# Attention with block sums and a gated feed-forward layer: other filling products for TensorE, and a new written-out order

## The chip, the cores and the metric

The kernel runs on one core of a Trainium2 chip. The metric is the device time in microseconds of one execution, as the median of a few runs. Profiles come from one profiled execution, whose own time is given beside them.

## The reference

```python
def _attn_ref(q, k, v):                 # (4, 8, 768, 64) each
    k_sum = k.reshape(B, H, nb, 32, D).max(axis=3)
    v_sum = v.reshape(B, H, nb, 32, D).mean(axis=3)
    scores_l = scale * np.matmul(q, k.transpose(0, 1, 3, 2))
    mask_l = np.abs(pos[:, None] - pos[None, :]) < 16
    scores_s = scale * np.einsum('bhsd,bhnd->bhsn', q, k_sum) + np.log(32)
    # softmax over [masked local scores, block scores], then times [v, v_sum]
    ...
def _moe_ref(x, w_in, w_out):           # x (3072, 512), d_ff 2048
    h = x @ w_in
    g = h * np.clip(h + 3.0, 0.0, 6.0) / 6.0
    return g @ w_out
```

Each query sees the keys less than 16 places away and one maximum of k (one mean of v) for each of 24 blocks. The heads' outputs side by side are x of the feed-forward layer, whose output in float32 is the result.

## The kernel before, in words

TensorE's products are in bfloat16 with float32 sums in PSUM. Work is cut by batch (4) and half of the sequence (384 rows): eight stages s = 0 to 7 of the feed-forward layer, each fed by the attention of one half.

The operations have names with a stage in them. For batch 0, `k0` to `k3` transpose k (L391) and take block maxima and copies on VectorE and ScalarE; `q0` and `q1` do so for the second half of q (L420), `q2` and `q3` for the first (L441, from the wide load `Q0w`). `s0p0` and `s0p1` are scores of a head pair (L489): those of the half that is done first begin with a product that writes the mask into PSUM, called cover (L481), which reads the identity (`c.1`, GpSimd, L250) and a bias (`c.3`, VectorE, L261). `u0` and `u1` sum v over blocks (L535). `v0p` are the values of a head pair with their division and transposes (L581, L589); `v4hg` and `vbhg` are those of later halves (L623, L636). For later batches `w` turns k and q into place with VectorE's transposes, `s` are scores of four heads at a time (L512), `u` sums of v (L553). `Fsxf` is the first product of the layer for stage s and slice f of d_ff (four L666 products of 384 columns; ScalarE's relu, L670; VectorE's gate, L671). `Gstxa` is the second (L683, sixteen products of 512 columns in four parts, then a copy and a store).

Nothing is scheduled at run time or by a planner in the file: `ORDER` is a written-out list of all operations. `Plan.issue` reads it word by word, gives an operation its buffers when it is first named (the one of its pool that was set free longest ago), and hands it to its engine. Every engine works its part of the list in that order, and waits where an operation needs something that isn't there. A suffix `:A` or `:D` names ScalarE or VectorE where both can do it. Loads are issued by GpSimd, stores and moves by SyncE, in the order of the list too.

Words that begin with a sign are filling products: `-n` is n products of 128 columns of ones, `~n` n products of 512, into a PSUM buffer that is free. Nobody reads them. They stand where TensorE would wait, mostly in the first 23 us.

Of the kernel before, what the change touches and what calls it, by code (L numbers as in the profile page):

```python
# [36 lines left out]
s011.1 F0x4.2 F0x4.3 F0x4.4 s011.2 F0x4.5 I8.0 F0x8.0 F0x8.1 F0x8.2 F0x5.0 I0.0 F0x1.0 F0x1.1 v410.0 v410.1 v410.2 c.12:A F0x5.1  # L37
F0x5.2 F0x1.2 F0x1.3 F0x1.4 F0x11.0 F0x11.1 F0x11.2 F0x1.5 F0x7.0 F0x7.1 F0x7.2 v411.3 I12.0 F0x15.0 F0x15.1 F0x15.2 v411.4:D
F0x13.0 F0x13.1 F0x13.2 v410.3 v410.4:A F0x14.0 F0x10.0 F0x14.1 F0x14.2 F0x10.1 F0x10.2 I2.0 F0x3.0 F0x3.1 F0x3.2 F0x3.3 F0x3.4
F0x3.5 F1x4.0 F1x4.1 F1x4.2 F0x0.0 F0x0.1 F0x0.2 F0x0.3 F0x9.0 F1x2.0 F0x2.0 F0x2.1 K11.0 K10.0 K12.0 K13.0 w10.0 F0x0.4 F0x9.1  # L40
F0x9.2 F1x2.1 F0x2.2 F1x2.2 F0x0.5 F1x12.0 F1x12.1 F1x12.2 Q1w4.0 Q1w5.0 Q1w1.0 F1x5.0 F1x5.1 F1x5.2 F1x9.0 F1x9.1 F1x9.2 F0x2.3
F0x2.4 F0x2.5 F1x8.0 F1x8.1 F1x8.2 F0x6.0 F0x6.1 F0x6.2 F1x6.0 F1x6.1 F1x6.2 w11.0 Q1w3.0 q5.0 F1x14.0 q5.1:A F1x14.1 F1x14.2
F1x15.0 F1x15.1 F1x15.2 w11.1:A F1x1.0 Q1w2.0 Q1w0.0 q7.0 q7.1:A w11.2 w10.1:D w10.2 w11.3:D w10.3:D q6.0 q6.1:A F1x7.0 F0x12.0
F0x12.1 F0x12.2 q4.0 q4.1:A O0.0 F1x7.1 F1x1.1 G02x0.0 O1.0 G02x0.1 F1x1.2 F1x7.2 s100.0 s100.3 s100.1 F1x3.0 w13.0 w12.0 F1x3.1
F1x0.0 F1x0.1 F1x0.2 F1x11.0 w12.2 w12.3:D w13.2 w13.3:D s100.4 s101.0 s101.1 s101.3 O2.0 O3.0 F1x3.2 s100.2 G02x0.2 G02x0.3
G02x0.4:A w13.1:A w12.1:A F1x10.0 s101.4 G00x0.0 G00x0.1 V10.0 h100.0:A F1x11.1 s101.2 F1x11.2 h110.0:D V12.0 h130.0:D s110.0
s110.3 s110.1 G00x0.2 G00x0.3 G00x0.4:A h120.0:D s110.2 F1x10.1 u4.0 u4.1:A u4.3:D u4.2:A u4.4:D G01x0.0 G01x0.1 G01x0.2
h101.0:A h121.0:A v100.0 u4.5:D s110.4 G02x0.5 v101.0 G01x0.3 G01x0.4:A F1x10.2 F1x13.0 v100.1 v100.2 v100.3 h111.0:A G12x0.0
v101.1 v101.2 v100.4:A v101.3 v101.4:A F1x13.1 h131.0:A K21.0 G12x0.1 G12x0.2 K20.0 K22.0 K23.0 w20.0 w20.3 w21.0 F1x13.2 w21.3
# [752 lines left out]
```

## Time and profile before

| | us |
|---|---|
| median of 3 runs | 220.14 (218.53 to 221.66) |
| profiled execution, its own time | 221.35 |
| its span, first to last instruction | 219.6 |
| TensorE products busy | 212.7 (97%) |
| VectorE busy | 164.0 (75%) |
| ScalarE busy | 135.9 (62%) |
| GpSimd busy | 50.0 (23%) |

PE is TensorE's products, PEld its weight loads, DVE VectorE, ACT ScalarE, POOL GpSimd, SP SyncE. Each product has a weight load ahead of it that counts as an instruction of its own. Products are pipelined, and a product's end is modelled, so a busy TensorE need not be at its peak; how far apart products start says more. PEclk is the share of full clock that TensorE was granted. In the chain of waits, "issue" is time in which an engine waited for nothing that the profile shows.

### The profile page before, as it was taken

Reading aid. Unit: us, or ns where it says so; the run is one execution under the profiler, and the core shown is the slowest. Engines: PE = TensorE matmul, PEld = TensorE weight load, DVE = VectorE, ACT = ScalarE, POOL = GpSimd, SP = SyncE. Lnnn points to the kernel's source line nnn. Section 1 sums busy time; section 2 is a strip of 40 time slices with the busy share of each in tenths; the row PEclk is TensorE's granted clock in tenths of the full one; section 3 lists DMA queues with packets and bytes.
Section 4 is the critical chain, followed back from the end, with each engine's and each line's share of the span. In section 5 each row is a group of like instructions: output and inputs, shape, how many; then the busy total and the mean of one; then the engine's idle time right before and its main releaser. Section 6 shows DMA issues by size and latency. Waiting matters only on the chain.

```text
span 219.6 us, 6084 instructions
## 1 busy us (share of the span) xinstructions
PE 212.7 (97%) x2546; PEld 122.3 (56%) x2546; DVE 164.0 (75%) x311; ACT 135.9 (62%) x270; POOL 50.0 (23%) x66
## 2 busy tenths in 40 slices
PE   7998999999999999999999999999999999999993
PEld 7566666655445556555545555555555555554442
DVE  5888589997999999999989999968966666421111
ACT  8579497787897878893857687377244555510110
POOL 7977447824630007600000000000000000000000
PEclk9999579999999999999999999999999999999999
DMA  5999999999999915999333134023233200021332
GB/s 69 149 155 188 204 186 158 202 199 162 177 186 173 102 48 35 165 210 138 36 39 146 17 37 116 3 30 63 33 34 36 100 0 4 0 96 72 123 132 105
DMA packets 91580, 22.68 MB, mean 103 GB/s; under 512 B 82208, under 2 KB 88608, under 8 KB 91552
## 3 DMA queue, kind: packets, MB, share of 16 engines
q0 software_dynamic: 62288, 14.41, 70.8%
q1 hardware_dynamic: 29264, 7.87, 15.0%
q8 instruction: 20, 0.33, 0.6%
q14 instruction: 8, 0.07, 0.1%
HBM read 28.82 MB, written 6.29 MB: 160 GB/s over the span
## 4 chain that ended last, share of the span: by engine, by line
PE 89%; DVE 4%; DMA 3%; issue 1%; POOL 1%; ACT 1%; POOLq 0%
PE h L666 37%; PE o L683 31%; PE h L683 5%; DMA first<-in_k_dram 3%; PE S L623 3%; PE S L512 2%; PE S L489 1%; PE h L581 1%; PE S L666 1%; PE S L553 1%; PE S L636 1%; DVE at L521 1%; DVE vaug L241 1%; PE S L481 1%; DVE red L467 1%
## 5 line engine op out<-in xcount | busy, mean ns | idle before, releaser
L666 PE MATMUL h<-x,win 128*128 128x384 bf16 x496 | 90.5, 328 | 0.0
L670 ACT ACTIVATE r<-h 128x384 f32<-128x384 f32 x124 | 58.7, 491 | 37.2 <-PE h L666 36.7
L683 PE MATMUL o<-wout,g 128*128 128x512 bf16 x336 | 81.0, 380 | 0.0
L671 DVE SCALAR_TENSOR_TENSOR g<-r,h 128x384 bf16<-128x384 f32 x124 | 65.5, 548 | 20.4 <-ACT r L670 17.8
L666 PEld LDWEIGHTS <-win 128*128 128x128 bf16 x512 | 48.8, 98 | 35.3 <-issue 0.3
L683 PEld LDWEIGHTS <-g 128*128 128x128 bf16 x400 | 38.1, 98 | 38.4 <-issue 0.2
L520 ACT ACTIVATE at<-S 120x768 bf16<-120x768 f32 x24 | 18.7, 809 | 3.6 <-PE S L512 3.5
L343 POOL DMA_DIRECT2D vaug<-in_v_dram x10 | 11.8, 1186 | 20.6 <-PE S L623 18.2
L241 ACT COPY ot<-o 128x512 f32<-128x512 f32 x15 | 8.8, 586 | 11.2 <-PE o L683 11.2
L521 DVE TENSOR_TENSOR at<-at,mask 96x768 bf16<-96x768 bf16 x24 | 12.9, 546 | 1.2 <-ACT at L520 0.7
L241 DVE COPY ot<-o 128x512 f32<-128x512 f32 x6 | 4.1, 690 | 12.6 <-PE o L683 12.6
L605 DVE TENSOR_TENSOR xn<-S,rc 128x768 bf16<-128x768 f32 x14 | 13.2, 948 | 0.3
L683 PE MATMUL h<-wout,g 128*128 128x256 bf16 (+1 forms) x64 | 11.9, 326 | 0.0
L241 ACT COPY ot<-h 128x512 f32<-128x512 f32 (+1 forms) x2 | 1.0, 478 | 17.5 <-PE h L683 17.5
L467 DVE TENSOR_REDUCE red<-kaug 128x24 bf16<-128x768 bf16 x12 | 11.1, 934 | 0.1
L455 DVE STREAM_TRANSPOSE kaug<-kraw 128x768 bf16<-128x768 bf16 x8 | 8.1, 1028 | 1.1 <-PE S L512 1.1
L770 PEld LDWEIGHTS <-idle 128*128 128x128 bf16 x78 | 7.2, 127 | 2.9 <-DVE idle L287 1.1
L770 PE MATMUL o<-idle 128*128 128x128 bf16 (+1 forms) x55 | 7.4, 327 | 1.1 <-DVE idle L287 1.1
L241 ACT COPY vaug<-vaug 32x640 bf16<-32x640 bf16 (+3 forms) x17 | 8.3, 535 | 0.1
L642 DVE STREAM_TRANSPOSE y<-xn 128x768 bf16<-128x768 bf16 x8 | 7.7, 968 | 0.1
L512 PEld LDWEIGHTS <-kaug 32*128 32x128 bf16 x576 | 5.3, 93 | 4.2 <-issue 3.4
L623 PEld LDWEIGHTS <-at 120*64 120x64 bf16 x336 | 6.5, 114 | 2.1 <-issue 1.1
(108 smaller groups left out, 198.2 us busy)
## 6 DMA issues: line engine op xcount, KB each, us to landing
out_dram<-ot SPq DMA_DIRECT2D x19, 256.0 KB, 3.1
vaug<-in_v_dram POOLq DMA_DIRECT2D x6, 384.0 KB, 13.5
wout<-in_moe_w_out_dram POOLq DMA_DIRECT2D x4, 512.0 KB, 10.0
win<-in_moe_w_in_dram POOLq DMA_DIRECT2D x3, 512.0 KB, 10.3
kraw<-in_k_dram POOLq DMA_DIRECT2D x8, 192.0 KB, 12.6
x<-y SPq DMA_DIRECT2D x64, 24.0 KB, 2.0
first<-in_k_dram POOLq DMA_DIRECT2D x6, 192.0 KB, 14.6
first<-in_q_dram POOLq DMA_DIRECT2D x6, 192.0 KB, 11.5
```

What stands on the lines that cost most here:

```text
L241: {"ACT": nc.scalar.copy, "DVE": nc.vector.tensor_copy, "POOL": nc.gpsimd.tensor_copy}[eng](o, i)
L343: op("POOL", "dma128", lambda: nc.gpsimd.dma_start(out=o[BLK:WIN, a:z, 0:D], in_=rows[:, a:z]), w=[("v", b % 2, c) for c in range(lo, hi)] ...
L467: op("DVE", "max", lambda: nc.vector.tensor_reduce(red.slot[:], w[:, :, BLK:WIN].rearrange("p t (n c) -> p t n c", n=2), axis=AX.X, op=ALU ...
L520: op("ACT", "exp", lambda a=a, e=e: nc.scalar.activation(a, X[e].slot[0:KEYS, :, 0:HALF], AF.Exp, scale=scl), r=[X[e]], w=[("at", p, half)])
L521: op("DVE", "masking", lambda m=m: nc.vector.tensor_tensor(m, m, mask[:, low(half):low(half) + HQ].unsqueeze(1).to_broadcast([WIN, 2, HQ, ...
L605: nc.vector.tensor_tensor(o, src[..., 0:D], r.unsqueeze(len(r.shape)).to_broadcast(list(o.shape)), op=ALU.mult)
L623: nc.tensor.matmul(X.slot[64 * c:64 * c + 64, i, m:m + D + 1], a[:, t * QB:(t + 1) * QB], vaug[b % 2][0:KEYS, h, t, 0:D + 1], start=True, ...
L666: nc.tensor.matmul(bank(h)[:, 0:HALF], w_in_sb[:, kt, cols], xt[s].slot[:, kt], start=(kt == 0), stop=(kt == NP - 1))
L670: op("ACT", "relu", lambda: nc.scalar.activation(r.slot[:], bank(h)[:, 0:HALF], AF.Relu, bias=0.5, scale=1.0 / 6.0), r=[h], w=[r])
L671: op("DVE", "gate", lambda: nc.vector.scalar_tensor_tensor(gt[s].slot[:, ft], r.slot[:], 1.0, bank(h)[:, 0:HALF], op0=ALU.min, op1=ALU.mul ...
L683: nc.tensor.matmul(o.slot[:, a:z], gt[s].slot[:, ft, ts * 128:(ts + 1) * 128], w_out_sb[:, ft, a:z], start=(ft == 0), stop=(ft == NFT - 1))
L770: nc.tensor.matmul(o[:, 0:m * 128].rearrange("p (m c) -> p m c", m=m), idle[:], idle[:].unsqueeze(1).to_broadcast([128, m, 128]), start=Tr ...
```

## The change

Three things are changed.

1. `ORDER` is another list of the same operations. It differs from the first word to the last. Ahead of `k1`, `-44` has become `_36 -19` and two covers, `s010.0 s000.0`; the identity `c.1` now stands ahead of q's first load on GpSimd; the fill ahead of `k2` is `=8` five times and `=3` instead of `~11`; other fills have become `=` words too, and there are more of them up to `q3`.
2. Two more filling words: `_n` is n products of 64 columns, and `=n` is one product in float32 of 32 n columns, on the same ones read as float32 (`idle` is made 256 wide for that).
3. The transposes of wide q for batch 1 have a name of their own (`qwtr4`), which changes no instruction.

The diff, its lists cut to their beginnings and ends:

```diff
 ORDER = """
-c.0 c.6 K01.0 c.19 c.9:A c.10:A c.5 c.8:D c.18 c.7 c.14:A c.15:A c.17 c.11:A K00.0 K02.0 c.2 c.4 c.20 Q00.0 c.13:D c.1 -44 k1.0
-c.3 k1.1 k1.4 Q01.0 k1.2:D c.16 k0.0 k0.3:A k0.2:A k1.3:A k0.1 k0.4 ~11 k2.0 k2.3:A k3.0 k3.1 k2.1 ~2 q0.0 q0.2:A k3.4 k2.2:D
-q0.1:A s010.0 ~1 -1 s010.1 s010.2 q1.0 q1.2:D s000.0 k3.2:A V00.0 h000.0:D q1.1:D k3.3:D s000.1 s000.2 s030.0 -3 s030.1 s030.2
-V01.0 ~1 -1 u0.0 u0.1:A h010.0:D k2.4 v00.0 -3 v00.1 u0.3:A -1 v01.0 v01.1 v00.2 v00.3 u0.4:D h001.0:A h011.0:A v01.2 v01.3
-s020.0 s020.1 s020.2 V03.0 V02.0 u1.0 h030.0:D h031.0:D -2 v01.4 h020.0:D v01.5:D u1.3:A u1.4:A -2 v03.0 Q0w2.0 -4 v03.1 v03.2
-v03.3 Q0w1.0 v00.4 Q0w0.0 -2 q3.0 q3.1:D v00.5:D u1.1:A u1.2:D h021.0:A q2.0 q2.1:A v02.0 v02.1 v02.2 v02.3 s021.0 v03.4 v03.5:D
-s031.0 s021.1 s021.2 s031.1 s031.2 I4.0 F0x4.0 F0x4.1 s001.0 v02.4 s011.0 v02.5:D s001.1 s001.2 v411.0 v411.1 v411.2 u0.2:A
...
-G60x0.3 G60x0.4:D G60x0.5 G71x0.2 G71x0.3 G71x0.4:A G71x0.5
+c.0 K01.0 c.7 c.15:A c.5 c.6 c.9:A c.18 K00.0 c.11:A c.10:D c.13:D K02.0 c.14:A c.8:D c.20 c.2 c.3 c.1 _36 -19 s010.0 s000.0 c.4
+c.19 c.16 c.17 k1.0 k1.3:D k1.1 k1.4 k0.0 Q00.0 k0.2:A k0.3:A k1.2:A k0.1 k0.4 =8 =8 =8 =8 =8 =3 k2.0 k2.3:A k3.0 k3.1 k3.4 k2.1
+k3.3:D =8 q0.0 q0.1:A q0.2:A =8 =6 s000.1 s000.2 =4 s010.1 s010.2 Q01.0 q1.0 =3 s030.0 k2.2:D k2.4 V00.0 h000.0:D h001.0:D V01.0
+=8 =8 =1 u0.0 u0.3:D u0.1:D s020.0 q1.2:A k3.2:A s030.1 q1.1:A h010.0:A h011.0:A s020.1 s020.2 V02.0 u0.4:D h020.0:D v01.0 v01.1
+v00.0 v01.2 v01.3 V03.0 v00.1 v00.2 v00.3 u1.0 h030.0:D u1.3:A h031.0:D s030.2 u1.4:D h021.0:A v01.4 v01.5:D Q0w1.0 Q0w0.0
+Q0w2.0 u1.1:A =8 =8 =8 =3 q3.0 q3.1:D q2.0 u1.2:D v03.0 q2.1:A v03.1 v03.2 s021.0 s021.1 v03.3 v02.0 v02.1 v02.2 v02.3 s011.0
+s011.1 v00.4 v00.5:D v03.4 v03.5:D =2 v02.4 v02.5:A s021.2 s011.2 s031.0 s001.0 I2.0 F0x3.0 s031.1 s031.2 F0x3.1 F0x3.2 F0x3.3
+F0x3.4 F0x3.5 I4.0 F0x6.0 F0x6.1 F0x6.2 F0x4.0 F0x4.1 F0x4.2 v411.0 s001.1 v411.1 s001.2 u0.2:A v411.2 F0x4.3 F0x4.4 F0x4.5
...
+G60x0.4:A G60x0.5 G70x0.0 G70x0.1 G60x0.0 G72x0.1 G72x0.2 G70x0.2 G70x0.3 G70x0.4:A G50x0.5 G60x0.1 G60x0.2 G60x0.3 G60x0.4:D
+G70x0.5 G60x0.5 G72x0.3 G72x0.4:D G71x0.2 G71x0.3 G72x0.5 G71x0.4:A G71x0.5
 """
...
-            if token[0] in "~-":
-                keep(int(token[1:]), 4 if token[0] == "~" else 1, min(...))
+            if token[0] in "~-_=":
+                keep(int(token[1:]), "-~_=".index(token[0]), min(...))
...
-    idle = sb([128, 128], BF16, "idle")
+    idle = sb([128, 256], BF16, "idle")
...
-        op("PE", "qwtr", tr, ...)
+        op("PE", "qwtr4" if b else "qwtr", tr, ...)
...
     def keep(n, m, o):
         o = o[:, 0] if any(o is x for x in pairs) else o[:]
+        if m == 3:
+            w = idle[:].bitcast(F32)
+            nc.tensor.matmul(o[:, 0:32 * n].rearrange("p (n c) -> p n c", n=n), w, w[:, 0:32].unsqueeze(1).to_broadcast([128, n, 32]), start=True, stop=True)
+            return
+        c = (2, 8, 1)[m]
         for _ in range(n):
-            nc.tensor.matmul(o[:, 0:m * 128].rearrange("p (m c) -> p m c", m=m), idle[:], idle[:].unsqueeze(1).to_broadcast([128, m, 128]),
+            nc.tensor.matmul(o[:, 0:c * 64].rearrange("p (c x) -> p c x", c=c), idle[:, 0:128], idle[:, 0:64].unsqueeze(1).to_broadcast([128, c, 64]),
                              start=True, stop=True)
```

More of the change, by code (lines that the diff above doesn't have):

```diff
@@ L38 @@
[L38 to L49, printed above, removed]
@@ new lines @@
+F0x11.2 v410.2 c.12:A F0x7.0 F0x7.1 F0x7.2 v411.3 I12.0 F0x15.0 F0x15.1 F0x15.2 F0x13.0 F0x13.1 F0x13.2 v410.3 K13.0 v410.4:A
+v411.4:D F0x10.0 F0x10.1 F0x10.2 F0x14.0 F0x14.1 F0x9.0 F0x9.1 F0x2.0 F0x14.2 F0x0.0 F0x0.1 F0x0.2 F0x0.3 F0x2.1 F0x0.4 K11.0
+K10.0 K12.0 w10.0 F0x9.2 F1x14.0 F1x14.1 F1x14.2 F1x1.0 F1x1.1 F0x2.2 F0x2.3 F0x2.4 F1x1.2 F0x2.5 F0x0.5 F1x5.0 F1x5.1 F1x5.2
+F1x4.0 F1x4.1 F1x4.2 F1x2.0 F1x2.1 F1x2.2 w10.2 w10.3:D Q1w5.0 Q1w0.0 Q1w1.0 Q1w2.0 q7.0 q7.1:A q6.0 q6.1:A F1x7.0 F1x7.1 F1x7.2
@@ new lines @@
+F2x5.1 F2x5.2 s111.3 w22.3 F2x3.0 F2x3.1 F2x3.2 G12x0.3 G12x0.4:A w23.0 F2x9.0 F2x9.1 F2x9.2 s111.4 s111.1 F2x12.0 F2x12.1
+F2x12.2 G10x0.0 w23.2:A F2x11.0 F2x11.1 K32.0 H2.0 h131.0:A V20.0 V22.0 H2.1:D G10x0.1 s111.2 Q20.0 K31.0 w23.3 F2x15.0 F2x15.1
+F2x15.2 F2x11.2 F2x13.0 u5.0 u5.1:A F2x13.1 v111.0 v110.0 w23.4:A w21.4:A u5.2:A F2x10.0 F2x4.0 G10x0.2 G10x0.3 w20.4:A F2x13.2
+G02x0.5 Q22.0 Q32.0 v111.1 F2x2.0 u5.5:D v110.1 v110.2 G01x0.5 G12x0.5 G00x0.5 K33.0 Q23.0 w20.1 v111.2 u5.3:D w21.1 w22.2:A
@@ new lines @@
+G10x0.4:A G10x0.5 v110.3 w22.4:A F2x2.1 F2x10.1 v110.4:A F2x10.2 G11x0.0 G11x0.1 F2x4.1 F2x4.2 u5.4:D w22.1 K30.0 v111.3
+v111.4:A F2x2.2 G11x0.2 G11x0.3 G11x0.4:A F3x0.0 F3x0.1 F3x0.2 w23.1 F3x8.0 F3x8.1 F3x8.2 s200.0 s200.1 s200.3 s200.4 G22x0.0
+F3x7.0 F3x7.1 F3x7.2 F2x14.0 F2x14.1 F2x14.2 s210.0 s200.2 F3x13.0 F3x4.0 F2x8.0 s210.3 s210.4 s210.1 s210.2 G22x0.1 F3x13.1
+F3x13.2 F3x4.1 F3x4.2 F2x8.1 F2x8.2 v201.0 v201.1 v200.0 v200.1 v200.2 F3x6.0 F3x6.1 F3x6.2 G22x0.2 G22x0.3 G22x0.4:A F3x2.0
@@ new lines @@
+F3x2.1 w21.5:A v200.3 v201.2 w20.5:D v201.3 F3x3.0 F3x12.0 F3x3.1 F3x12.1 F3x12.2 s201.0 F3x2.2 F3x3.2 V32.0 H3.0 V30.0 H3.1:A
+Q30.0 Q33.0 Q31.0 w30.0 G20x0.0 w23.5:A s201.1 F3x14.0 F3x14.1 s201.2 G20x0.1 s201.3 F3x9.0 F3x1.0 G20x0.2 w31.0 F3x14.2 F3x9.1
+F3x1.1 F3x1.2 F3x9.2 G22x0.5 w30.3 G20x0.3 w22.5:A G20x0.4:A w31.2:A F3x11.0 F3x11.1 s211.0 s211.1 w32.0 w32.2:A s211.2 w32.3
+F3x11.2 s201.4 w33.0 F3x5.0 F3x5.1 F3x10.0 G21x0.0 G21x0.1 G21x0.2 G21x0.3 s211.3 s211.4 F3x5.2 w32.4:D F3x15.0 F3x15.1 u6.0
@@ new lines @@
+u6.1:D G21x0.4:A F3x10.1 w31.3 F3x15.2 F3x10.2 v211.0 u6.3:A u6.4:A v210.0 v210.1 v210.2 v210.3 v211.1 v211.2 w31.4:A w30.2:A
+v201.5 G32x0.0 G32x0.1 G32x0.2 G32x0.3 G32x0.4:A v201.4 v201.6 v201.7 F4x10.0 F4x10.1 F4x10.2 F4x11.0 v211.3 F4x14.0 F4x14.1
+F4x14.2 G21x0.5 G11x0.5 G30x0.0 F4x11.1 F4x11.2 G20x0.5 F4x3.0 G30x0.1 F4x3.1 F4x3.2 w31.1 F4x8.0 F4x8.1 F4x8.2 F4x1.0 F4x1.1
+u6.5:A w31.5:D F4x1.2 w30.1 w30.5:D F4x4.0 F4x4.1 F4x4.2 G30x0.2 F4x7.0 F4x7.1 G30x0.3 G30x0.4:A w33.2:A F4x5.0 w30.4:D w33.1
@@ new lines @@
+F4x7.2 F4x0.0 F4x0.1 F4x0.2 G31x0.0 G31x0.1 s300.0 w33.3 w32.1 w33.4:D F4x5.1 F4x5.2 u6.2:D s300.1 s300.2 s300.3 s300.4 F4x13.0
+F4x15.0 F4x15.1 G31x0.2 F4x13.1 F4x13.2 v211.7 v211.6 v211.5 s310.0 s310.3 s310.4 s310.1 s310.2 v211.4 F4x2.0 G31x0.3 F4x15.2
+F4x6.0 F4x6.1 F4x6.2 F4x2.1 G31x0.4:A F4x2.2 v301.0 v301.1 v300.0 F4x9.0 v301.2 F4x12.0 G42x0.0 F5x5.0 G42x0.1 G31x0.5 v301.3
+F4x9.1 F4x9.2 F4x12.1 F4x12.2 v300.1 v300.2 v300.3 v301.6 F5x5.1 F5x14.0 F5x14.1 w33.5:D F5x6.0 F5x6.1 F5x14.2 F5x5.2 F5x6.2
@@ new lines @@
+w32.5:D G42x0.2 G42x0.3 G42x0.4:A s301.0 s301.3 s301.1 F5x0.0 F5x0.1 F5x0.2 F5x8.0 F5x10.0 F5x10.1 F5x10.2 F5x8.1 s301.4 F5x8.2
+G40x0.0 s311.0 s311.3 F5x2.0 s311.4 F5x3.0 F5x12.0 G40x0.1 F5x3.1 F5x3.2 s301.2 s311.1 s311.2 G40x0.2 F5x12.1 F5x12.2 F5x2.1
+F5x2.2 v311.0 v310.0 v310.1 v310.2 G40x0.3 G40x0.4:A v311.1 F5x7.0 F5x7.1 v311.2 v310.3 F5x7.2 F5x4.0 F5x9.0 F5x9.1 F5x9.2
+G41x0.0 G41x0.1 F5x1.0 F5x1.1 F5x1.2 F5x11.0 v311.3 v301.5 F5x4.1 v301.7 v301.4 G30x0.5 F5x4.2 G41x0.2 F5x13.0 F5x13.1 F5x13.2
@@ new lines @@
+F5x11.1 F5x11.2 G41x0.3 G41x0.4:D G32x0.5 v311.6 F6x1.0 F6x1.1 F6x1.2 v311.7 v311.4 F6x4.0 F6x0.0 F6x4.1 F6x4.2 G52x0.0 F6x0.1
+F6x9.0 F6x9.1 F6x0.2 F5x15.0 F5x15.1 F6x5.0 F6x5.1 G52x0.1 F6x9.2 F6x5.2 F5x15.2 v311.5 F6x6.0 F6x6.1 F6x11.0 F6x11.1 F6x11.2
+F6x8.0 F6x8.1 F6x8.2 F6x6.2 G52x0.2 F6x12.0 F6x14.0 F6x14.1 F6x14.2 F6x10.0 F6x10.1 F6x10.2 F6x12.1 F6x12.2 G52x0.3 G52x0.4:A
+F6x7.0 F6x15.0 F6x15.1 F6x2.0 F6x15.2 F6x7.1 F6x7.2 G51x0.0 F6x3.0 F6x3.1 F6x2.1 G42x0.5 G40x0.5 F7x2.0 F7x2.1 F6x2.2 F6x3.2
@@ L139, in issue @@
         for n, token in enumerate(ORDER.split()):
-            if token[0] in "~-":
-                keep(int(token[1:]), 4 if token[0] == "~" else 1, min((s for p in ("o", "h", "S") for s in self.pools[p]), key=lambda s: since[id(s)]))
+            if token[0] in "~-_=":
+                keep(int(token[1:]), "-~_=".index(token[0]), min((s for p in ("o", "h", "S") for s in self.pools[p]), key=lambda s: since[id(s)]))
                 continue
@@ L441, in tr @@
                         nc.tensor.transpose(bank(T).bitcast(BF16)[:, at_:at_ + 128], src[:, p * 128:(p + 1) * 128], ident[:])
-        op("PE", "qwtr", tr, r=[("qw", b, (1 - half) * m + u) for u in range(m)] + ["ident"], w=[T])
+        op("PE", "qwtr4" if b else "qwtr", tr, r=[("qw", b, (1 - half) * m + u) for u in range(m)] + ["ident"], w=[T])
         lo = low(half) * QB
```

51 lines of the change are left out of this document (15 added, 36 removed).

## The prediction

> **What bounds the kernel now.** I read the page first: busy shares, the 40 slices, the chain that ended last.
>
> ```profile
> span 219.6 us, 6084 instructions
> PE 212.7 (97%) x2546; PEld 122.3 (56%) x2546; DVE 164.0 (75%) x311; ACT 135.9 (62%) x270; POOL 50.0 (23%) x66
> PEclk9999579999999999999999999999999999999999
> PE 89%; DVE 4%; DMA 3%; issue 1%; POOL 1%; ACT 1%; POOLq 0%
> ```
>
> TensorE bounds it: 89% of the chain is its own work. The 97% says little, since ends are modelled, so I compare one stretch with what its products cost. The groups of 35.00 to 216.24 us, then prices from the chain:
>
> ```profile
> L666 PE MATMUL h<-x,win 128*128 128x384 bf16 x472 | 85.5, 327 | 0.0
> L666 PE MATMUL S<-x,win 128*128 128x384 bf16 x12 | 2.6, 326 | 0.0
> L683 PE MATMUL o<-wout,g 128*128 128x512 bf16 x336 | 81.0, 380 | 0.0
> L683 PE MATMUL h<-wout,g 128*128 128x512 bf16 x32 | 7.6, 380 | 0.0
> 71.24 1.95 PE h L666 x12
> 69.51 1.73 PE o L683 x8
> 67.98 0.34 PE S L636 x6
> 47.43 0.78 PE S L439 x48
> 51.91 0.48 PE S L512 x48
> 65.48 0.88 PE S L623 x48
> 81.56 0.78 PE S L553 x48
> ```
>
> L666: 484 x 1.95/12 = 78.7 us. L683: 368 x 1.73/8 = 79.6 us. The 32 half-width L683 products, at half, 3.5 us. The small groups (576 of L512, 288 of L623, 144 of L553, 96 of L439, 30 of L636) come to 5.8 + 5.3 + 2.3 + 1.6 + 1.7 = 16.7 us. Together 178.5 of 181.24 us: after 35 us a new order can win at most about 2.7 us. What can be won otherwise lies before. The chain there, with the columns start, duration, what:
>
> ```profile
> 9.83 0.53 PE h L391 x16
> 11.71 0.43 PE S L481 x2
> 12.41 0.28 PE S L489 x12
> 15.12 0.72 PE h L535 x21
> 15.84 0.20 issue
> 16.91 0.31 PE h L581 x12
> 18.70 0.80 PE o L535 x24
> 21.07 1.44 issue
> 22.51 0.34 PE h L589 x3
> 28.42 0.87 PE S L623 x24
> 29.29 2.01 PE h L666 x10
> ```
>
> Twice TensorE stands at "issue", where no semaphore, engine or transfer explains it. Counting instructions does. Stretches with the counts of products and weight loads, then the packets that carry instructions (the whole page, and the stretch 20 to 21.1 us):
>
> ```profile
> 0.00:15.95 15.95, 14.24 (x223) 10.30 (x223) 12.20 (x35) 11.61 (x22) 13.90 (x24) 1.00 1.34 124
> 15.95:21.50 5.55, 4.95 (x128) 3.71 (x128) 4.49 (x14) 4.92 (x11) 4.38 (x6) 1.00 1.80 183
> 23.01:29.83 6.82, 6.79 (x118) 4.71 (x116) 4.78 (x12) 4.64 (x6) 2.97 (x4) 0.50 1.38 198
> q8 instruction: 20, 0.33, 0.6%
> q8 instruction: 1, 0.02, 5.5%
> ```
>
> 446 instructions stand before the first stop and exactly 256 between the stops. The 20 packets hold 0.33 MB, 16.5 KB each, for 5,092 TensorE instructions: 255 a packet. So TensorE's program comes in blocks of 256, and both stops are at a block's edge (446 and 702; the edge before is 190, about the eighth transpose pair of k2, 9.9 us). Edge to edge it took 9.9 to 16.04 and 16.04 to 22.51: 6.1 and 6.5 us. I read it so: entering a block orders the next one, which is there about 6.3 us later while the other queue is full. The stop at 21.07 then has a second cost: the third window row shows a granted clock of 0.50 from 23.01 to 29.83.
>
> **The Trainium skill against this.** "Runtime: NRT & Kernel Launch", section Instruction fetch mechanics, also has blocks of 256 instructions, but calls the cost of crossing an edge "one DMA tail-bump, mostly hidden". By that rule the 1.44 us has another cause, and an earlier edge wins nothing; this is a rival below.
>
> **The change part by part.** The warming fill ahead of k1 and the fill ahead of k2:
>
> ```profile
> 1.13 4.88 PE L770 MATMUL o<-idle 128*128 128x128 bf16 x44 [1.13 <-DVE idle L287]
> 6.28 0.88 PE L391 MATMUL h<-ident,first 96*64 96x96 bf16 x32 [0.28 <-POOL ident L250]
> 7.09 2.55 PE L770 MATMUL o<-idle 128*128 128x512 bf16 x11
> 4.17 0.74 POOL L312 DMA_DIRECT2D first<-in_q_dram  x1
> 5.20 1.03 POOL L250 TENSOR_SCALAR_AFFINE_SELECT ident<-ident 128x128 bf16<-128x128 bf16 x1
> 5.90 0.18 DVE L261 TENSOR_SCALAR bias<-band 96x384 bf16<-96x384 bf16 x1
> 2.77 7.02 DMA first<-in_k_dram
> ```
>
> - *36 narrow and 19 plain products for 44 plain ones.* One plain product takes 4.88/44 = 0.111 us. A 64-column one has no row: between 0.055 (by columns) and 0.111 (no gain). 19 x 0.111 + 36 x (0.055 to 0.111) ends the fill between 5.2 and 7.2 us. Columns set the price in all warm rows, so I take 0.06 and 5.4 us.
> - *ident and bias earlier.* On GpSimd the identity now stands ahead of q's first load: from the end of that load's issue, 4.91, to the identity's, 6.23, are 1.3 us; from 4.17 on that gives 5.5. That load is issued 1.3 us later, but the load of k ahead of it on the queue lands at 9.79, so it starts no later. VectorE's bias (5.90 before) loses the mask copy ahead of it and its wait, gains one memset, and is ready at about 5.5 too.
> - *Two covers (L481) moved ahead of k1.* They wait for ident and bias, and k1 and k0 wait behind them on TensorE, then VectorE's and ScalarE's copies of k. 2 x 0.43 from 5.6 us, then the two transposes at about 0.37 each: the k fill starts at 7.3, not 7.09. Hidden by the wait for k's third load; 0.2 us without that.
> - *Float32 fill.* A unit is 32 columns, 43 units ahead of k2, 118 in all. The compiled program has two loads and two products for each float32 product, 23 of them. For 8 units (256 columns) no row exists. Below: 256 columns of bfloat16 once, 2.55/11/2 = 0.116 us. Above: the two loads exposed as well, 0.75 us. Twice the bytes and two products make 4 x 0.107 = 0.43 us, the middle of the bounds; I take that. Ahead of k2: 5.4 x 0.43 = 2.3 us, so it is done at 9.6 and k2 starts with its load as before, 9.83.
> - The skill's "FP8 and Floating Point Precision", TensorE Precision Notes, has four passes for float32; by it the sum is the same. No row here shows one.
> - *From k2 to u0.* The covers' 0.86 us have gone, fills of 31 units (1.65 us) stand there instead of 0.6 to 1 us; u0 starts at about 15.0, as before.
> - *Block edges.* Counted in the new order, with four instructions for a float32 product: 110 of fill, 8 of covers and 64 of k1 and k0 stand ahead of the k fill, so edge 190 falls in its second product, 7.9 us instead of 9.9. The second block's successor is there at 14.2 and u0 no longer stops: edge 446 is crossed in the middle of u0 at 15.4, not 16.04. Edge 702 falls into q2; the third wait ends at 15.4 + 6.3 = 21.7, not 22.51. TensorE reaches it at about 21.0: u0's rest, two covers or scores, v01, v00, u1 and a fill of 27 units (1.44 us) ahead of q3, which also covers the wait for wide q. So a stop of 0.7 us stays. Without the fill the same stop would be 2 us, which is what it hides.
> - *Then, at full clock,* q2's rest 0.3, v03 and v02 at 0.62 each, four scores at 0.28, three transposes at 0.17, one wait for v02's scaling 0.3: first layer's F0x3 starts at 25.2. Eleven L666 products (1.79 us) end at 27.0, in v411 edge 958 is reached, and the block is there at 21.7 + 6.3 = 28.0. A new stop of 0.8 us.
>
> *The sum.* Both orders have then done the same attention work. Before, v411 starts at 28.42 with two L666 products behind it, and by 29.83, at half clock, it brings v411 (0.44) and two more (0.33): 1.10 us done, by full-clock prices. After, 1.92 at 28.0 and 1.83 more by 29.83: 3.75. The lead is 2.65 us. The profiled execution took 221.35 us (span 219.6 and 1.75 around it), above the median 220.14: 221.35 - 2.65 = 218.7. A run of the kernel before without the half clock would itself stop at its edge 958 until 22.51 + 6.3 = 28.8, with 1.5 us done; the lead over that is 1.2 us. If the fastest run, 218.53, is such a run, after takes 217.3. I take the middle, **218.0 us**. The new order from 35 us on I set at zero, between the 2.7 us that can be won and as much lost.
>
> **The rivals.**
> 1. *The lead is given back on VectorE* (220.8 us, chance 0.10). For it: its slices from 30 to 130 us.
>
> ```profile
> 30.00:130.00 100.00, 99.84 (x1337) 56.34 (x1335) 92.96 (x161) 78.08 (x157) 28.58 (x33) 1.00 1.25 127
> ```
>
> VectorE is busy 92.96 of 100 us there. A lead of 2.65 us needs that much of its 7.0 idle us; against it, work on L683 can be put between, which needs no VectorE. If four fifths are lost, 0.5 us stay: 220.8.
>
> 2. *The edges cost nothing* (the skill's rule; 221, chance 0.06). Then "issue" at 21.07 is something else and comes again, the half clock with it, and only 0.2 to 0.5 us move. Against it: exactly 256 instructions between two stops.
>
> 3. *The new order also wins after 35 us* (215.3, chance 0.18): all of the 2.7 us on top of the forecast. For it: the order was changed in every part. Against: sixteen stages of scores and values keep their own starting gaps, whatever the order.
>
> 4. *Slower: float32 fill does not count as work for the clock* (225, chance 0.11). The clock fell for 6.82 us after a stop of 1.44 us, so an idle share of that size is enough. If the fills count as idle, the stretch from 9.8 to 21.7 holds mostly them: useful work there is about 6.9 us (k, q, two covers, four scores, two sums, two values, q3), and half clock adds up to that: 218.7 + 6.9 = 225.6. It decides from five sixths of that stretch on (224.5). Against it: useful products fill more than half of it.
>
> **How the numbers follow.** Forecast 0.55 (own range 216.0 to 220.4), rivals 0.10, 0.06, 0.18 and 0.11. Beyond 2% (4.4 us, about what a measurement of this kernel tells from no change): faster is rival 3 and a little of the forecast's edge, 0.20; slower is rival 4, 0.11; within 2% the rest, 0.69. The range leaves out rival 4 and the outer part of rival 3: 214.5 to 222.4.
>
> **What would show it.** Right: edge 190 near 7.9 us and k2 still at 9.8; no stop in u0; stops at 21 to 21.7 and at 27 to 28 of about 0.7 us, each 256 instructions after the last; granted clock 1.00 from 6 us on; float32 products 0.4 us each. Wrong: a k2 later than 10.2 (the fill is too dear), a slice of half clock between 10 and 30 us (rival 4), VectorE without idle time and TensorE waiting for it after 40 us (rival 1), a stop of 1.4 us away from an edge (rival 2). The prediction falls if TensorE's first L666 product starts later than 26.2 us, as before.

## The result, and the profile after

| | before | after |
|---|---|---|
| median, 20 runs each | 220.29 (218.49 to 223.86) | 218.59 (218.29 to 219.48) |
| ratio, 95% interval | | 0.9938 (0.9914 to 0.9961) |
| profiled execution, its own time | 221.35 | 218.39 |
| its span | 219.6 | 216.7 |

By the ratio the change gains 0.6%, by the medians 0.8%; both lie within the 2% that count as no change. Medians here hold all runs of a kernel; ratios leave out runs over 1.5% above the kernel's fastest, which in the experiments below are all runs that lost some of their clock. What has gone with the change is the spread: the slowest run of after is quicker than the median of before.

The page of after: span, busy shares, granted clock, packets of instructions, chain.

```profile
span 216.7 us, 6117 instructions
PE 211.0 (97%) x2561; PEld 124.0 (57%) x2561; DVE 161.5 (75%) x315; ACT 135.8 (63%) x266; POOL 50.1 (23%) x66
PEclk9999999999999999999999999999999999999999
q8 instruction: 20, 0.33, 0.6%
PE 93%; ACT 2%; DVE 2%; issue 1%
```

The two slices of half clock have gone from PEclk. TensorE's own work is 93% of the chain, not 89%. Its timeline in the first 30 us (start, duration, operation, count, idle before it):

```profile
1.26 3.82 PE L775 MATMUL o<-idle 128*128 128x64 bf16 x55 [1.26 <-DVE idle L287]
5.71 0.81 PE L481 MATMUL S<-bias,ident 96*128 96x384 bf16 x4 [0.63 <-DVE bias L261]
7.39 2.62 PE L771 MATMUL o<-idle 128*128 128x256 f32 x12
9.96 0.53 PE L391 MATMUL h<-ident,first 96*64 96x96 bf16 x16
15.97 0.85 PE L535 MATMUL h<-vaug,ind 96*32 96x128 bf16 x24
19.97 1.71 PE L771 MATMUL S<-idle 128*128 128x256 f32 x8
21.52 0.50 PE L441 MATMUL S<-ident,qwide 128*128 128x128 bf16 x6
27.37 0.31 PE L623 MATMUL S<-vaug,at 120*64 120x65 bf16 x7
27.84 0.47 PE L623 MATMUL S<-vaug,at 120*64 120x65 bf16 x17 [0.15 <-issue]
```

No stop is left at 21 us: ones stand ahead of q3 until 21.5, and the edge is crossed at 21.97 without a wait. A short one came at 27.49 to 27.84, 256 instructions later.

**Two executions of before.** A second profile of the unchanged kernel (`b_again`, 218.52 us) had the stop and not the half clock. Its page, and below it its timeline:

```profile
span 216.8 us, 6084 instructions
PEclk9999999999999999999999999999999999999999
```

```profile
14.78 0.85 PE L535 MATMUL h<-vaug,ind 96*32 96x128 bf16 x24
20.09 0.38 PE L581 MATMUL h<-vf,at 24*64 24x65 bf16 x12
21.71 0.34 PE L589 MATMUL h<-ident,xn 128*128 128x128 bf16 x3 [1.25 <-issue]
26.54 1.15 PE L666 MATMUL h<-x,win 128*128 128x384 bf16 x6
28.00 0.81 PE L666 MATMUL h<-x,win 128*128 128x384 bf16 x4 [0.31 <-issue]
```

So the half clock is not in every run of before. The records of the runs give a mean granted clock for each. Of 103 runs of before made beside the experiments, 39 had 0.995 or more, median 219.12 us; 52 had less than 0.99, median 221.10. All 20 runs of after had 0.997 or more. (Edge times below are counted in the records of the traces, loads and products together. A stop is the time from the start of the last instruction ahead of it to the start of the first behind it; the idle time in the brackets of a row counts from the last one's modelled end and is shorter.) The medians then split roughly so: about 0.5 us of the gain is there against a run of before at full clock (219.12 to 218.59), and the other 1.2 us goes with the runs of before that lost some of their clock. Which part of the new list the 0.5 us comes from, no run here isolates.

**The work done by 30 us.** The groups of TensorE's first-layer products (L666) and second-stage values (L623) from 0 to 30 us, first of the profiled run of before, then of `b_again`, then of after:

```profile
L666 PE MATMUL h<-x,win 128*128 128x384 bf16 x5 | 1.8, 469 | 0.0
L623 PE MATMUL S<-vaug,at 120*64 120x65 bf16 x24 | 0.9, 244 | 0.0
```

```profile
L666 PE MATMUL h<-x,win 128*128 128x384 bf16 x13 | 2.8, 327 | 0.3 <-issue 0.3
L666 PE MATMUL S<-x,win 128*128 128x384 bf16 x4 | 1.0, 329 | 0.0
L623 PE MATMUL S<-vaug,at 120*64 120x65 bf16 x48 | 1.1, 196 | 0.4 <-ACT at L495 0.4
```

```profile
L666 PE MATMUL h<-x,win 128*128 128x384 bf16 x20 | 3.6, 327 | 0.0
L623 PE MATMUL S<-vaug,at 120*64 120x65 bf16 x36 | 1.2, 199 | 0.2 <-issue 0.2
```

At the prediction's prices (1.95/12 and 0.88/48 us) after leads the first by 15 x 0.1625 + 12 x 0.0183 = 2.66 us, and the second by 3 x 0.1625 - 12 x 0.0183 = 0.27 us. The spans end 2.9 and 0.1 us apart, so nearly all of the difference is made before 30 us.

### The profile page after: what moved, and what is told of

It is laid out like the page before. It is cut to its first block, busy times and chain, and to the rows that moved or that the text cites. A ratio compares the mean times of both kernels' runs of the same rounds, so it can differ in the third digit from the quotient of the medians.

```text
span 216.7 us, 6117 instructions
## 1 busy us (share of the span) xinstructions
PE 211.0 (97%) x2561; PEld 124.0 (57%) x2561; DVE 161.5 (75%) x315; ACT 135.8 (63%) x266; POOL 50.1 (23%) x66
## 4 chain that ended last, share of the span: by engine, by line
PE 93%; ACT 2%; DVE 2%; issue 1%
PE h L666 38%; PE o L683 33%; PE h L683 5%; PE S L623 3%; PE S L512 3%; ACT vaug L241 2%; PE h L771 2%; PE o L771 1%; PE h L581 1%; PE S L553 1%; DVE vaug L282 1%; PE S L636 1%; PE S L666 1%; PE S L771 1%; PE S L489 1%
## 5 line engine op out<-in xcount | busy, mean ns | idle before, releaser
L666 PE MATMUL h<-x,win 128*128 128x384 bf16 x500 | 90.9, 326 | 0.0
L666 PEld LDWEIGHTS <-win 128*128 128x128 bf16 x512 | 48.7, 98 | 35.6
L241 ACT COPY ot<-o 128x512 f32<-128x512 f32 x18 | 10.5, 585 | 15.2 <-PE o L683 15.0
L343 POOL DMA_DIRECT2D vaug<-in_v_dram x10 | 12.4, 1250 | 10.9 <-PE S L623 10.6
L241 DVE COPY ot<-o 128x512 f32<-128x512 f32 x3 | 2.1, 689 | 14.6 <-PE o L683 14.6
L683 PE MATMUL h<-wout,g 128*128 128x256 bf16 (+1 forms) x64 | 11.2, 326 | 0.0
L241 ACT COPY ot<-h 128x256 f32<-128x256 f32 (+1 forms) x3 | 1.3, 443 | 11.8 <-PE h L683 11.8
L623 PEld LDWEIGHTS <-at 120*64 120x64 bf16 x336 | 6.3, 111 | 2.9 <-issue 2.2
L333 POOL DMA_DIRECT2D kraw<-in_k_dram x8 | 6.2, 775 | 6.8 <-DVE kaug L455 4.4
L623 PE MATMUL S<-vaug,at 120*64 120x65 bf16 x336 | 7.4, 196 | 0.2 <-issue 0.2
```

What stands on the lines that cost most here:

```text
L241: {"ACT": nc.scalar.copy, "DVE": nc.vector.tensor_copy, "POOL": nc.gpsimd.tensor_copy}[eng](o, i)
L343: op("POOL", "dma128", lambda: nc.gpsimd.dma_start(out=o[BLK:WIN, a:z, 0:D], in_=rows[:, a:z]), w=[("v", b % 2, c) for c in range(lo, hi)] ...
L623: nc.tensor.matmul(X.slot[64 * c:64 * c + 64, i, m:m + D + 1], a[:, t * QB:(t + 1) * QB], vaug[b % 2][0:KEYS, h, t, 0:D + 1], start=True, ...
L666: nc.tensor.matmul(bank(h)[:, 0:HALF], w_in_sb[:, kt, cols], xt[s].slot[:, kt], start=(kt == 0), stop=(kt == NP - 1))
L683: nc.tensor.matmul(o.slot[:, a:z], gt[s].slot[:, ft, ts * 128:(ts + 1) * 128], w_out_sb[:, ft, a:z], start=(ft == 0), stop=(ft == NFT - 1))
```

## The experiments

Each lists its median (range, runs), its ratio to before on the same chip, and how many runs had a granted clock of 0.995 or more.

**Head or tail.** `h1_head_after` is after's list up to F0x1, then the operations that are left in before's order; `h2_head_before` the other way round. No filling words behind the cut.

```diff
 # h1: ORDER = after's words up to F0x1.5, then
-F0x11.0 F0x11.1 F0x11.2 v410.2 c.12:A F0x7.0 ...
+v410.2 c.12:A F0x11.0 F0x11.1 F0x11.2 F0x7.0 ...
 # h2: ORDER = before's words up to F0x1.5, then
-F0x7.0 F0x7.1 F0x7.2 v411.3 I12.0 ...
+I2.0 F0x3.0 F0x3.1 F0x3.2 ...
```

> The changed kernel's list up to its first five slices of stage 0 (F0x1, about 31 us), then what is left in the order of the kernel before. Theory 1 (the gain lies in the first 30 us: instruction blocks, clock): median about 218.9 us, 0.3 above the changed kernel's 218.6, and no half clock. Theory 2 (the gain lies in the new order after 30 us): about 220.3, as before.

> The other way round: the list of the kernel before up to F0x1, then what is left in the changed order. Theory 1: about 220.0 us, with the stop of 1.4 us near 21 us and, in part of the runs, a stretch at half clock, so a wide spread as before. Theory 2: about 218.6 and a narrow spread.

`h1`: 218.99 us (218.41 to 220.47, 12), 0.9942 (0.9910 to 0.9975), 12 of 12 runs at full clock. `h2`: 220.86 us (218.47 to 223.47, 12), 1.0030 (0.9988 to 1.0072), 4 of 12. The head carries the gain. Beside the median of after, `h1` says that after's tail wins 0.4 us; beside before on the same chip (220.42), `h2` says that it loses 0.4. So the tail is worth nothing that these runs can tell.

**The same kernel again**, for the spread of its traces:

> The kernel before, unchanged, for a second profile. Theory 1: stops at the 446th and 702nd instruction again, about 0.2 and 1.4 us. If this execution is a quick one (219 us or less), no stretch at half clock, and instead a stop at the 958th instruction, near 28.8 us, of up to 1.5 us. Rival (the stops are no block edges): they lie elsewhere or are gone in a quick run.

218.52 us (1); its rows are shown above. Edge 702 had its stop again (1.43 us), edge 446 had none this time, and edge 958 had one of 0.63 us. The stop at edge 702 does not halve the clock every time.

**The fill ahead of q3 taken out.**

```diff
-u1.1:A =8 =8 =8 =3 q3.0
+u1.1:A q3.0
```

> The changed kernel without the fill of 27 units (1.55 us) ahead of q3. Theory 1: TensorE reaches edge 702, now in v03, at about 20.9 us and stops there until 22.0, since the block comes when it comes; nothing else is late, so 218.6 where the clock stays full. The stop of about 1.1 us makes a stretch at half clock possible, as in the kernel before: then 219.5 to 220 and a wide spread. Rival (the fill itself costs its 1.55 us): 217.1.

219.35 us (218.52 to 220.88, 10), 0.9972 (0.9929 to 1.0015), 4 of 10 at full clock; those four have a median of 218.62, like after. Its timeline, its granted clock on the page, and the busy times of 24.43 to 27.84 us (the clock is the third number from the end):

```profile
20.88 0.28 PE L581 MATMUL h<-vaug,at 96*64 96x65 bf16 x5 [0.24 <-ACT at L495]
21.97 0.31 PE L581 MATMUL h<-vaug,at 96*64 96x65 bf16 x7 [0.80 <-issue]
```

```profile
PEclk9999799999999999999999999999999999999999
```

```profile
24.43:27.84 3.41, 3.41 (x36) 1.92 (x36) 2.15 (x6) 1.93 (x4) 0.89 (x2) 0.50 1.32 205
```

The stop is back, 0.99 us long, and it ends at 21.97, when after crosses the same edge too. The ones win no time at the edge itself; they keep the clock, as expected. This is the clearest of the experiments.

**The fill ahead of u0 taken out.**

```diff
-V01.0 =8 =8 =1 u0.0
+V01.0 u0.0
```

> The changed kernel without the fill of 17 units ahead of u0. In its profile u0 starts at 15.97 us, and ScalarE's copy h010 waits for u0 and holds v01 until 17.79. Theory 1: u0 starts at 15.0, block edge 446 is crossed 0.9 us earlier, so the later blocks are there earlier: the stop at edge 958 stays under 0.4 us and the end comes 0.6 to 0.9 us earlier, 217.8. Rival: copies on VectorE and ScalarE set v01, or the later fill and the blocks eat it: 218.6.

218.47 us (218.27 to 218.97, 9), 0.9915 (0.9878 to 0.9952), all at full clock: nothing lost, nothing won. u0 stays where it was, with a wait instead of ones:

```profile
15.91 0.85 PE L535 MATMUL h<-vaug,ind 96*32 96x128 bf16 x24 [0.51 <-DVE vaug L241]
```

In the new order u0 waits for VectorE's copy of v until 15.9 us; in before it started at 15.1 (profiled run) and 14.78 (`b_again`).

**The narrow lead undone, or done alone.** `a_plain_lead` is after with 37 products of 128 columns ahead of k1; `b_narrow_lead` is before with after's 36 narrow and 19 plain ones.

```diff
 # a_plain_lead
-_36 -19 s010.0 s000.0
+-37 s010.0 s000.0
 # b_narrow_lead
-c.1 -44 k1.0
+c.1 _36 -19 k1.0
```

> The changed kernel with 37 plain products for the 36 narrow and 19 plain ones of the lead: the same columns, 36 instructions fewer. Theory 1 (blocks of 256, each about 6 us after the edge before): edge 190 falls into k2, at 10.2 us instead of 8.1; edge 446 into s030.1, at about 17.4, without a stop; edge 702 into v03's second half, with a stop of about 0.8 us until 23.4; 0.8 us slower, 219.4. Rival (the count of leading instructions is of no account): 218.6, stops where they were in the work.

> The kernel before with the 36 narrow and 19 plain products of after for its 44 plain ones, and nothing else: 22 more instructions of the same columns. Edge 190 moves from k2, which waits for k's third load (it was seen to start between 9.56 and 10.69 us), into the fill ahead of it, at about 9 us. Theory (an edge ahead of that wait frees the later edges from the load, but each edge also lies 22 instructions earlier in the work): edge 446 at 15.0 to 15.3 in every run, edge 702 reached at about 20 and its block there at 21.4, so the stop of 1.4 us stays and the half clock after it too, in about half of the runs. Runs without the half clock 218.6 to 219.1 (before 219.1), those with it 220.5 to 221.2, median 219.7. Rival (the narrow lead is what the change gains by): median 218.6 and no run with the half clock.

`a_plain_lead`: 218.68 us (218.26 to 220.35, 10), 0.9964 (0.9923 to 1.0006), all at full clock. Edge 190 moved from 8.15 to 10.04 us, as counted, but the 0.8 us did not follow: edges 446, 702 and 958 were crossed at 17.14, 22.53 and 28.28, a stop only at the last (0.52 us). The block behind edge 702 was there 5.39 us after edge 446, or sooner, where about 6 were expected. `b_narrow_lead`: 220.18 us (218.67 to 221.82, 12), 1.0007 (0.9967 to 1.0048), 8 of 12 at full clock. Its stop at edge 702:

```profile
20.36 0.21 PE L581 MATMUL h<-vf,at 24*64 24x65 bf16 x1
21.29 0.37 PE L581 MATMUL h<-vf,at 24*64 24x65 bf16 x11 [0.72 <-issue]
```

The block came earlier, as expected (21.29 us, 21.71 in `b_again`), but the edge lies 22 instructions earlier in the work too. The median was 0.5 us above the 219.7 expected, and the runs at full clock had 219.46 where 218.6 to 219.1 were expected. The narrow lead is not what the change gains by.

**Fewer instructions in the lead.** `b_wide_lead` has eleven products of 512 columns for before's 44 of 128; `a_wide_lead` nine of 512 and one of 128 for after's 55.

```diff
 # b_wide_lead
-c.1 -44 k1.0
+c.1 ~11 k1.0
 # a_wide_lead
-_36 -19 s010.0 s000.0
+~9 -1 s010.0 s000.0
```

> The kernel before with 11 products of 512 columns for its 44 of 128 in the lead: the same columns, 66 instructions fewer, so all block edges lie 66 instructions later in the work. Theory 1: edge 190 in q0 (11.4 us), edge 446 in v01 with a stop of about 0.2 us, edge 702 in v02's second half: the stop that was ahead of v00's transposes moves there, to about 22.7, and lasts about 1.1 us. Median within 0.7 us of the kernel before. Rival (no block edges): the stop stays ahead of v00's transposes.

> The kernel after with nine products of 512 columns and one of 128 for the 36 narrow and 19 plain ones that lead up to k: the same columns in 20 instructions instead of 110. Edge 190 moves from the k fill to q0 (about 11.3 us), edge 446 from u0 to v01 (17.5), 702 into v02 (23), 958 among the values of the second stage or later (28 to 29). Theory (the change's many narrow instructions push each edge earlier and gain nothing; fewer of them is better): no stop at 702 beyond 0.5 us, no stop at 958, and 0.3 to 0.6 us less than after: 218.0 to 218.3. Rival (where the edges lie is of no account once the half clock is kept away): 218.6, as after.

`b_wide_lead`: 217.98 us (217.3 to 220.12, 10), 0.9928 (0.9882 to 0.9974), 10 of 10 at full clock, the lowest median of all, though its interval overlaps that of after. The stop at edge 702 is where and as long as it was expected, and about as long as that of `a_q3_no_fill`; the time is not: it lies 1.9 us under before on the same chip (219.91), where at most 0.7 was expected.

```profile
22.24 0.24 PE L581 MATMUL h<-vf,at 24*64 24x65 bf16 x3
23.36 0.32 PE L581 MATMUL h<-vf,at 24*64 24x65 bf16 x9 [0.87 <-issue]
```

It lies 66 instructions further in the work than before's, and no run lost the clock. `a_wide_lead`: 218.62 us (218.36 to 219.19, 12), 0.9932 (0.9900 to 0.9964), all at full clock, as its rival had it: 90 instructions fewer win nothing on after.

**Ones in place of the stop.** `b_fill_stop` puts 1.4 us of ones into before ahead of the stop at edge 702, `b_wide_fill` 0.93 us into `b_wide_lead`.

```diff
 # b_fill_stop
-Q0w2.0 -4 v03.1
+Q0w2.0 -4 ~6 v03.1
 # b_wide_fill (also with ~11 for -44)
-q2.1:A v02.0
+q2.1:A ~4 v02.0
```

> The kernel before with six filling products of 512 columns (about 1.4 us) ahead of `v03.1`, so that ones stand where TensorE stood still for 1.43 us ahead of v00's last products. They add 12 instructions ahead of edge 702, and the block behind the edge isn't there sooner. Theory (the stop costs little by itself, since the same work ends at 28 us with it and without it; what it costs is that the clock sometimes falls to half after it): the work is no earlier than in the single run of before at 218.52, but no run has the half clock, so the median falls to 218.3 to 218.9 and the highest run to under 220. Rival (the gain of the change comes from its order and its earlier covers): the kernel stays at the 220.3 of before, or 0.3 above it for the added products.

> The kernel before with eleven products of 512 columns for the 44 of 128 (the 217.98 us of an earlier run) and with four more of 512 columns (0.93 us) ahead of `v02.0`, where that kernel stood still for 1.07 us at edge 702. Theory: the stop becomes filling work, the half clock has no idle stretch to follow, the work is no earlier: median 217.6 to 218.0 and no run above 219. Rival (the ones end later than the block comes): 0.3 us more than without them, 218.3.

`b_fill_stop`: 219.93 us (218.82 to 225.24, 12), 0.9985 (0.9947 to 1.0023), 11 of 12 at full clock. `b_wide_fill`: 218.30 us (217.93 to 220.08, 12), 0.9925 (0.9892 to 0.9957), 11 of 12. In the first the clock did what the theory said in all but one run (225.24 us) and the median did not: 219.79 for the eleven runs, 0.4 us above before's full-clock runs on the same chip (219.40). `b_wide_fill` lies 0.3 us above `b_wide_lead`, as its rival had it. The profiled run of `b_fill_stop` (220.8 us):

```profile
10.69 0.53 PE L391 MATMUL h<-ident,first 96*64 96x96 bf16 x16 [1.05 <-DMA first<-in_k_dram]
21.33 1.69 PE L770 MATMUL S<-idle 128*128 128x128 bf16 x10
27.82 0.57 PE L623 MATMUL S<-vaug,at 120*64 120x65 bf16 x24 [0.35 <-ACT at L495]
29.30 1.46 PE L666 MATMUL h<-x,win 128*128 128x384 bf16 x8 [0.91 <-DVE rc L598]
```

Here k's third load came 0.9 us later than in the profiled run of before, edge 190 lies behind that wait, and edges 446, 702 and 958 were crossed at 17.08, 23.28 and 29.30, each 6.0 to 6.2 us after the last. (The row at 29.30 names VectorE as what ended the wait; the block came at about the same time, so either can have.) One profile doesn't say how much of the 0.4 us is the load and how much the ones; that stays open.

**Bfloat16 ones for float32 ones**, of four times the columns.

```diff
-=8    -=6      -=4   -=3 -=2 -=1
+~2    +~1 -2   +~1   +-3 +-2 +-1
```

> The changed kernel with each float32 filling product replaced by bfloat16 ones of four times its columns (8 units by two products of 512, 3 units by three of 128, and so on); four more instructions in all. Theory 1 (float32 is only a way to fill): the same within 0.3 us, 218.6. Rival (float32 fills better or cheaper): 219.5 or more, with stops or half clock.

218.78 us (217.97 to 220.2, 10), 0.9942 (0.9903 to 0.9982): the same as after. That float32 is used is of no account. The profiled run (220.2 us, the slowest of the ten) is one in which the clock came late: its covers took 1.44 us where after's took 0.81, and its fill ahead of k2 ended at 11.9 us, two later:

```profile
5.71 1.44 PE L481 MATMUL S<-bias,ident 96*128 96x384 bf16 x4 [0.32 <-DVE bias L261]
8.50 3.51 PE L775 MATMUL o<-idle 128*128 128x512 bf16 x13
```

## Why the prediction was right, and where not

The time came out at 218.59 for 218.0 forecast, within the range of the likeliest case. By the steps:

- *Lead at 29.83 us against the profiled run:* forecast 2.65 us, measured 2.66 at 30 us; the span of after ended 2.9 us earlier. The size is right; the way to it less so (Edges, below).
- *Lead against a run without the half clock:* forecast 1.2, measured 0.27. This is the term that was mis-sized, and why the middle of 218.7 and 217.3 came out 0.6 us too low. It failed on before's side alone. Carried on to 30 us, the forecast has 3.92 us of work done in after and 2.7 in before; measured by the groups above are 3.91 and 3.64. I took before's block behind edge 702 at 22.51 and the next at 28.8; in `b_again` they came at 21.71 and 28.00, because edge 446 did not stop there (15.34 instead of 16.04).
- *The profiled run stood for the kernel before.* It was one of two kinds: 39 of 103 runs of before kept all of their clock, with a median of 219.12. I took a middle without knowing the shares; that it came out within 0.6 us is in part luck.
- *The lead up to k:* forecast to end at 5.4; it did at 5.08. 36 narrow products took (3.82 - 1.9)/36 = 0.053 us and the 19 plain ones 0.10, in the groups by shape:

```profile
L775 PE MATMUL o<-idle 128*128 128x64 bf16 x36 | 2.1, 241 | 1.3 <-DVE idle L287 1.3
L775 PE MATMUL o<-idle 128*128 128x128 bf16 x19 | 1.9, 283 | 0.0
```

- *Ident and bias at 5.5, fill from 7.3, edge 190 at 7.9, k2 at 9.83:* the covers started at 5.71, the fill at 7.39, edge 190 was at 8.15, k2 at 9.96. All within 0.25 us. The fill, not the load, ends last ahead of k2 now.
- *Float32 fill, 0.43 us for 8 units:* 0.47. The chain of after has its 43 units as

```profile
7.46 2.55 PE o L771 x12
```

  so 2.55/43 x 8. That is 4.1 times the 0.116 us of the same columns in bfloat16; the Trainium skill's "FP8 and Floating Point Precision", TensorE Precision Notes, has four passes, and this agrees. The bounds of 0.116 and 0.75 held it, though the 0.75 had no row behind it.
- *u0 at 15.0, as before:* wrong, 15.97. I had read it from TensorE's own row alone. In the new order VectorE copies v for it later, as `a_u0_no_fill` shows. What the 0.9 us cost is not known, since the lead by 30 us is the one forecast.
- *Edges:* 446 at 15.4 without a stop: it was 16.32, without a stop. 702 to be reached at 21.0 with a stop of 0.7 until 21.7: TensorE crossed it at 21.97 without a stop. 958 with a stop of 0.8 until 28.0: 0.35 until 27.84. First L666 at 25.2: 25.48. Two errors met here. u0 was 0.9 us late, and the blocks came sooner than in the 6.3 us I counted with: 702 at most 5.65 us after 446, 958 5.87 after 702. From 16.32, 6.3 us would have put edge 702 at 22.6. That the sum at 28 us is nearly the one forecast is luck to that extent. The two stops of about 0.7 us that were named as signs did not come; there was none at 21 us and one of half that at 27.8.
- *What the fill ahead of q3 is worth:* I had it hide 1.44 us of a 2 us stop. Without it the edge is crossed at the same time (21.97); it is worth the clock.
- *After 35 us, zero:* from 30 us on the lead over the profiled run grew by 0.3 us, that over `b_again` fell by 0.2, and `h1` and `h2` put the tail at 0.4 either way. Right to that size, and rival 3 falls.
- *Rival 1, the lead given back on VectorE:* not as described. From 30 to 130 us it is still busy for nearly as long (92.96 before), and the lead over the profiled run stays:

```profile
30.00:130.00 100.00, 99.91 (x1334) 56.38 (x1329) 91.97 (x163) 78.25 (x155) 29.52 (x32) 1.00 1.28 130
```

- *Rival 2, the edges cost nothing:* falls. Stops of 1.63 us (before) and 1.43 (`b_again`), 1.07 (`b_wide_lead`), 0.99 (`a_q3_no_fill`) and 0.93 (`b_narrow_lead`) moved with the count of 256 through v00, v02 and v03. The Trainium skill's "Runtime: NRT & Kernel Launch", Instruction fetch mechanics, calls such an edge mostly hidden; in the first 31 us here the runs disagree. The traces also hold the packets that carry the instructions (queue q8, 16 KB each), and they show what the stops wait for. Of the edges 446, 702 and 958 in the 14 traces, 20 were crossed behind a stop of over 0.3 us, and each of these stops ended 1.26 to 1.57 us after its packet had landed (in before, landed at 14.78 and 21.08, stops over at 16.04 and 22.51). None of the others was crossed sooner after its packet. That it is the loads on the other queue that make the packets late was not tested.
- *Rival 4, float32 does not count as work for the clock:* falls. After kept 1.00 in all the stretch from 5 us on, and its runs 0.997 or more. Its premise, that a stop of 1.44 us is enough for half clock, does not hold either: `b_again` had one of 1.43 us and kept 1.00.

Which stops cost the clock the experiments settle only in half. In the 73 runs of after, `h1`, `a_u0_no_fill`, `a_plain_lead`, `a_wide_lead` and `a_bf16_fill`, whose traces show no stop over 0.6 us near 21 us, all kept 0.997 or more. In before, `a_q3_no_fill` and `b_narrow_lead`, with stops of 0.9 to 1.6 us at 20.3 to 22.5 us, a third to over half of the runs lost some. But `b_wide_lead` with 1.07 us at 22.3 lost none, and the trace of `h2_head_before`, which shares before's head, has its half clock from 19.00 us on, ahead of that stop. So the stop alone does not decide.

A count in the traces, made after all the runs and tested by none, goes further. The stretches of granted clock are whole multiples of 3.413 us: 17.07 us at full and then 6.83 at half clock in before, 20.48 and 3.41 in `a_q3_no_fill`, 13.65 and 6.83 in `h2_head_before`. So I cut every trace into windows of 3.413 us that start where its full clock starts, and counted the work that starts in each window: the columns of each product, times the share of the 128x128 array that its weights fill, as a share of what full products at L666's 0.1625 us would do. (Float32 columns count twice, as they take twice as long.) The table has the four windows with the least work, and two that hold a stop.

| window at full clock | work in it | clock after it |
|---|---|---|
| `a_q3_no_fill`, 21.02 to 24.43 us | 0.30 | 0.50 |
| before, 19.59 to 23.01 | 0.30 | 0.50 |
| `h2_head_before`, 15.58 to 19.00 | 0.32 | 0.50 |
| `b_wide_fill`, 15.12 to 18.54 | 0.34 | 1.00 |
| `b_wide_lead`, 20.15 to 23.56 (its stop) | 0.39 | 1.00 |
| `b_again`, 19.41 to 22.83 (its stop) | 0.39 | 1.00 |

Of the 785 windows at full clock that end before 200 us, the three with the least work are the only three that half clock follows. So it seems to be the work in a window that counts, and not the stop alone: values with 24x64 or 96x64 weights fill little of the array, ones with 128x128 fill all of it. The windows lie differently in each execution (full clock starts at 5.94 us in before, 5.76 in `b_again`, 3.95 in `a_q3_no_fill`), which would make two kinds of runs out of one kernel. If the windows are moved over each trace to 100 places, none falls under 0.34 from 5 to 39 us in after, `h1`, `a_plain_lead`, `a_wide_lead` and `b_wide_lead`, and none of their 64 runs lost clock; in `b_again` some window is under 0.32 to 0.34 at 29 to 51 of the 100 places, and 64 of before's 103 runs lost some. It does not fit everywhere: in `b_fill_stop` it would be 39 to 45 places, and one run of 12 lost some.

## What to carry to other kernels

Count TensorE's instructions, loads included: where a stop has no releaser and lies at a multiple of 256 from the last, filling work ahead of it does not bring the work forward, but can keep the clock. Profile the kernel before more than once and look at the granted clock of every run: what looked like 2.65 us here was 2.66 against one kind of run and 0.27 against the other. Try the plainest edit beside the elaborate one: wider products in one fill of the lead gave at least as much as the whole new list.

## What the runs showed of the hardware that was not expected

- The same kernel, with a stop of 1.4 to 1.6 us at the same instruction near 21 us, kept its clock in one profiled execution and had 0.50 for 6.82 us in another; over 103 runs 39 had 0.995 or more, median 219.12 us, and 52 less than 0.99, median 221.10.
- A stop of 0.99 us was followed by 3.41 us at half clock (24.43 to 27.84 in `a_q3_no_fill`), half as long as in before; all such stretches ahead of 200 us last one or two times 3.413 us, and the windows of that length ahead of them hold the least work of all (0.30 to 0.32 of full).
- From the crossing of one edge to the first instruction behind the next stop it took 5.7 to 6.5 us wherever TensorE stopped for over 0.3 us at the next one before 31 us (before 6.05 and 6.5, `b_again` 6.4 and 6.3, after 5.9, `a_q3_no_fill` 5.8, `a_u0_no_fill` 5.7, `b_wide_lead` 6.0, `b_fill_stop` 6.2 and 6.0). It is no fixed time: in `a_plain_lead` edge 702 was crossed 5.39 us after 446 without a stop.
- The stops end 1.26 to 1.57 us after a 16 KB packet of instructions has landed.
- In executions whose first loads are the same, k2 started between 9.56 us (`b_again`, straight behind the fill) and 10.69 (`b_fill_stop`, behind a wait of 1.05 us for k's third load); an edge behind that wait moves with it.
